# A fused top-k attention and MLP kernel: another order of the work inside each step

## Chip, cores and metric

The kernel runs on one core of one Trainium2 chip. The metric is the device time of one execution in microseconds. Before the change it is 1720.72 us, the median of three runs (1718.17 to 1720.84).

## What is computed

The reference is an attention over 64 heads (batch 8, 8 heads, 576 tokens, head size 64) that keeps only the 32 largest scores of each row, followed by an MLP with a leaky ReLU over all 4608 tokens. All of it is in float32; the MLP's weights arrive as float64 words.

```python
scores = scale * np.matmul(q, k.transpose(0, 1, 3, 2))        # 8 x 8 x 576 x 576
kth = np.partition(scores, -32, axis=-1)[..., -32:-31]
scores = np.where(scores >= kth, scores, -1000000000.0)
scores = scores - np.max(scores, axis=-1, keepdims=True)
attn = np.exp(scores)
attn = attn / (np.sum(attn, axis=-1, keepdims=True) + 1e-09)
x = np.matmul(attn, v)                       # then (B,H,S,D) -> (B*S, H*D) = 4608 x 512
h = x @ w_in                                 # 512 x 2048
out = np.maximum(0.01 * h, h) @ w_out        # 2048 x 512
```

## The kernel before

**Units.** Attention is cut into 144 units. A unit is 128 query rows of one pair of heads (both heads, 576 keys each), or the 64 rows left over in two pairs of heads. `scores` (L170) multiplies queries and keys on PE into PSUM and ACT copies the result to SBUF (`s_sb`, L186). `top_k` (L188) runs on DVE in four rounds: a round takes the eight largest of each row for both heads (two MAX8, L195) and, except in the last round, replaces them by a very low number (two MATCH_REPLACE8, L198). `mask` runs on POOL (L207 to L211): everything below the 32nd largest gets a large negative term. `exponents(u, i)` on ACT (L214) takes the exponential of head i with the row's sum; `sums` on ACT (L219, tile `ze`) adds 1e-9; `reciprocals` on DVE (L223, tile `rz`) inverts; `normalize(u, i)` on ACT (L226) multiplies head i by it. `transpose_main` (L234) and `transpose_tail` (L240) transpose the weights on PE through PSUM, with copies on ACT (L235, L241, tile `wT`). `weigh_values` (L262) multiplies by the values on PE and copies the result into the token tiles `x` (L272).

**MLP.** The tokens are cut into chunks: eight of 128 tokens, then fourteen of 256. A chunk can begin when all its units are weighed. The first product goes to `ph` (L282, 256 tokens) or `pr` (L305, 128 tokens, with transposes `pg`, L298), each in two rotating PSUM buffers that transposes and the second product share; ACT applies the leaky ReLU (Prelu, L288 or L311) into `gT`. The second product is `pz` (L333), copied by ACT (L343) and stored by a DMA on SP's queue. The MLP is written as a generator that stops every few matmuls; `mlp_steps(budget)` takes pieces from it until a budget of PE columns is used up.

**Steps.** The order of all work is written out by hand, in a loop over steps s (from L456). Step s runs the four rounds of top k for unit s (`cur`), one in each of `slot(0)` to `slot(3)`; masks and exponentials for unit s-1 (`old`); reciprocal, normalization and transposes for unit s-2 (`older`). In every odd step PE also does a group: scores for unit s+2, the values of units s-3 and s-2, scores for unit s+3. Each engine works through its own queue in this written order and waits there for what it needs from others. Seven calls of `mlp_steps` in each step, the MLP slots below, spread the MLP between these pieces. `slot_budget` divides what is ready evenly over the slots until the next chunk is ready, with a factor of 0.71 in odd steps and 1.29 in even ones.

**Start.** After the first four units there is a gap of six steps without top k (steps 4 to 9). In it `convert()` turns the weights from float64 words into float32, in 16 pieces, partly on DVE and partly on ACT; `slot(1)` to `slot(3)` begin one piece each, and beginning a piece first ends the one before the last.

Of the kernel before, what the change touches and what calls it, by code (L numbers as in the profile page):

```python
# [17 lines left out]
def kernel(  # L18
# [113 lines left out]
    def load_qk(pi):  # L132
        qt = loads.tile([P, S], F32, name="qt")
        kt = loads.tile([P, S], F32, name="kt")
        nc.sync.dma_start(qt, qT[pi])
        nc.sync.dma_start(kt, kT[pi])
        qk_of[pi] = qt, kt

    def load_v(pi):
        v_of[pi] = loads.tile([P, NKC, 2, D], F32, name="vt", bufs=LOADED_V)  # L140
        nc.sync.dma_start(v_of[pi], vk[pi])
# [28 lines left out]
    def scores(u):  # L170
        ps = [ps_sc.tile([P, 2, 512], F32, name=f"psc{i}") for i in range(2)]
        for n in range(0, len(u.parts), 2):
            for half in range(2):
                for i, pi, side, r0 in u.parts[n:n + 2]:
                    qt, kt = qk_of[pi]
                    d = slice(side * D, (side + 1) * D)
                    nc.tensor.matmul(  # L177
                        ps[i][r0:r0 + u.rows, half, 0:HS],
                        qt[d, u.q0:u.q0 + u.rows],
                        kt[d, half * HS:(half + 1) * HS],  # L180
                        start=True, stop=True,
                    )
        u.both = work.tile([P, 2, S], F32, name="s_sb", bufs=6)
        u.s = [u.both[:, i, :] for i in range(2)]
        for i in range(2):
            nc.scalar.copy(u.s[i].rearrange("p (h n) -> p h n", h=2), ps[i][:, :, 0:HS])  # L186

    def top_k(u):  # L188

        u.tops = small.tile([P, 2, ROUNDS, 8], F32, name="tops")  # L190
        rest = [work.tile([P, S], F32, name=f"rest{i}", bufs=1) for i in range(2)]
        src = u.s
        for r in range(ROUNDS):
            for i in range(2):
                nc.vector.max(out=u.tops[:, i, r, :], in_=src[i])  # L195
            if r + 1 < ROUNDS:
                for i in range(2):
                    nc.vector.match_replace(out=rest[i], in_to_replace=u.tops[:, i, r, :],  # L198
                                            in_values=src[i], imm_value=LOWEST)
                src = rest  # L200
            yield
# [11 lines left out]
    def exponents(u, i):  # L213
        nc.scalar.activation(u.s[i], u.s[i], AF.Exp, bias=u.nbias[:, i:i + 1], scale=SCALE,  # L214
                             accum_out=u.z[:, i:i + 1])

    def sums(u):
        u.ze = small.tile([P, 2], F32, name="ze")
        nc.scalar.activation(u.ze, u.z, AF.Copy, bias=1e-9, scale=1.0)  # L219

    def reciprocals(u):
        u.rz = small.tile([P, 2], F32, name="rz")
        nc.vector.reciprocal(u.rz, u.ze)  # L223

    def normalize(u, i):
        nc.scalar.activation(u.s[i], u.s[i], AF.Copy, bias=0.0, scale=u.rz[:, i:i + 1])  # L226
# [93 lines left out]
    def mlp(ch):  # L320

        n = CHUNKS[ch]
        t0 = sum(CHUNKS[:ch])
        last_turn = None
        if n == P:
            last_turn = yield from hidden_of_tile(x_of[ch])
        else:
            yield from hidden_transposed(x_of[ch], n)
        for r0 in range(0, n, P):
            pz = ps_ml.tile([P, 512], F32, name="pz", tag="ml")  # L330
            for f in range(NFC):
                need_weights(HP * DFF // WCH + f // 2 + 1)
                nc.tensor.matmul(  # L333
                    pz[:, 0:DMODEL], gT[:, f, r0:r0 + P], w_out[f // 4][:, f % 4, :],
                    start=(f == 0), stop=(f == NFC - 1),
                )
                if f == 3 and last_turn:
                    last_turn()
                    yield 4 * TRANSPOSE
                if f % 2 and f + 1 < NFC:  # L340
                    yield 2 * DMODEL
            o_sb = work.tile([P, DMODEL], F32, name="o_sb", bufs=1)
            nc.scalar.copy(o_sb, pz[:, 0:DMODEL])  # L343
            nc.sync.dma_start(out[t0 + r0:t0 + r0 + P, :], o_sb)
            yield 2 * DMODEL
# [8 lines left out]
    def mlp_steps(budget):  # L354
        owed[0] += budget
        while owed[0] > 0:
            if running[0] is None:
                if not ready:
                    owed[0] = 0.0
                    return  # L360
                running[0] = mlp(ready.pop(0))
            cost = next(running[0], None)
            if cost is None:
                running[0] = None
            else:
                owed[0] -= cost
                backlog[0] -= cost
# [14 lines left out]
    def unit(n):  # L382
        return steps[n] if 0 <= n < len(steps) else None
# [20 lines left out]
    def slot_budget(s):  # L404

        after = [at for at, _ in ready_at if at >= s]
        until = gap[-1] if s in gap else after[0] if after else s
        mean = backlog[0] / ((until + 1 - s) * SLOTS)
        if s in gap or until < s + 2:
            return mean  # L410
        return mean * (GROUPED if s % 2 else 2.0 - GROUPED)
# [5 lines left out]
    def fetch_weights():  # L417
        chunk = next(chunks, None)
        got = load_weights(*chunk) if chunk else None
        if got:  # L420
            raw_chunks.append(got)
# [6 lines left out]
    def convert():  # L428

        if len(converting) == 2 or not raw_chunks:  # L430
            for c in converting[:1]:
                next(converting.pop(0), None)
        if raw_chunks:
            begun[0] += 1
            converting.append(convert_weights(*raw_chunks.pop(0), on_vector=begun[0] % 2 == 1))
            next(converting[-1])
        fetch_weights()

    with tc.manual_schedule():
        last = {p: n for n, u in enumerate(steps) if u for p in u.pairs}  # L440
        for p in range(HP):
            load_qk(p)
            if p < 3:
                scores(units[p])
        for _ in range(3 if moe_w_in.dtype != F32 else DFF):
            fetch_weights()
        for p in range(HP):
            load_v(p)

        def load_more(s):  # L450

            for of, load, n, lag in ((qk_of, load_qk, LOADED, -2), (v_of, load_v, LOADED_V, LAG + 1)):
                while len(of) < NPAIR and (len(of) < n or last[len(of) - n] + lag <= s):
                    load(len(of))

        for s in range(len(steps) + LAG + 1):  # L456
            cur, old, older, new = unit(s), unit(s - 1), unit(s - LAG), ()
            if s % 2 and s not in gap:
                new = (units if s < FIRST else steps)[s + 2:s + 4]
            picks = top_k(cur) if cur else iter(())  # L460
            budget = slot_budget(s)

            def slot(n):
                next(picks, None)
                if s in gap and n:
                    convert()

            if older:
                reciprocals(older)
                normalize(older, 0)  # L470
                normalize(older, 1)
            slot(0)
            if old:
                mask(old, 0)
                mask(old, 1)
            mlp_steps(budget)
            mlp_steps(budget)
            if older:
                transpose_main(older, 0)
            slot(1)  # L480
            mlp_steps(budget)
            if older:
                transpose_main(older, 1)
                transpose_tail(older)
            mlp_steps(budget)
            if old:
                exponents(old, 0)
            slot(2)
            for u in new[:1]:
                scores(u)  # L490
            if s % 2:
                for u in (unit(s - LAG - 1), older):
                    if u:
                        weigh_values(u)
            for u in new[1:]:
                scores(u)
            mlp_steps(budget)
            mlp_steps(budget)
            if old:
                exponents(old, 1)  # L500
                sums(old)
            slot(3)
            mlp_steps(budget)
            attended(s)
            if s >= gap[-1]:
                load_more(s)
        mlp_steps(1e9)
# [53 lines left out]
```

## Time and profile before

| What | Before |
|---|---|
| median of three runs | 1720.72 us |
| profiled execution | 1719.7 us, its span 1717.8 us |
| mean granted clock of PE | 0.97 |
| PE busy | 1569.1 us (91%) |
| DVE busy | 1490.6 us (87%) |
| POOL busy | 1079.3 us (63%) |
| ACT busy | 1032.9 us (60%) |
| one MAX8, one MATCH_REPLACE8 | 748 ns, 743 ns |
| one exponential, one normalization | 778 ns, 769 ns |

The span reaches from the first to the last instruction; the profiled execution's own time is 1.9 us longer. A line such as "PE main L234 <- ACT s_sb L226: 78.1, 31, 12.1" says that the engine on the left waited for the one on the right 78.1 us in total, 31 times, at most 12.1 us. A line of the chain of waits says when a piece of the chain began, how long it lasted, which engine and line it was, and how many instructions it holds. In a line of the order of time the brackets hold idle time of that engine just before, and what ended it.

### The profile page before, as it was taken

How to read it: one execution, taken by the hardware profiler on the slowest of the kernel's cores; microseconds unless marked ns; L12 is line 12 of the kernel's file. 1: busy time of each engine (PE TensorE's matmuls, PEld its weight loads, DVE VectorE, ACT ScalarE, POOL GpSimd, SP SyncE). 2: the span in 40 equal slices, each digit the busy share in tenths (PEclk: the TensorE clock that was granted, in tenths of full speed). 3: DMA queues.
4: the chain of work that ended last, by engine and by line, in shares of the span. 5: the costliest groups of instructions: out<-in, count | busy, mean ns of one | idle time of the engine just before them, and what ended most of it. 6: DMA issues, size and time to landing. Idle time of an engine off the chain costs nothing.

```text
span 1717.8 us, 25394 instructions
## 1 busy us (share of the span) xinstructions
PE 1569.1 (91%) x9104; PEld 1022.0 (59%) x9104; DVE 1490.6 (87%) x3114; ACT 1032.9 (60%) x2261; POOL 1079.3 (63%) x726
## 2 busy tenths in 40 slices
PE   4454799999977999999999999999999999999999
PEld 3222455555544758585857575757576757576765
DVE  8999988888888999999998989999989899999910
ACT  4773665666665657565656565656565656566630
POOL 5205666666666676767676766676666666667720
PEclk9686899999989999999999999999999999999999
DMA  4351010100110001100110001000110010100000
GB/s 159 127 191 41 1 35 34 38 7 21 35 44 6 2 7 62 38 7 9 60 34 11 13 29 41 32 13 15 54 32 13 1 40 1 36 1 13 1 13 13
DMA packets 22462, 57.21 MB, mean 33 GB/s; under 512 B 2368, under 2 KB 2368, under 8 KB 21312
## 3 DMA queue, kind: packets, MB, share of 16 engines
q1 hardware_dynamic: 22336, 55.58, 9.5%
q8 instruction: 72, 1.18, 0.3%
q14 instruction: 54, 0.44, 0.1%
HBM read 46.14 MB, written 9.44 MB: 32 GB/s over the span
## 4 chain that ended last, share of the span: by engine, by line
PE 75%; DVE 16%; ACT 8%; DMA 1%; issue 0%; SPq 0%; ACTq 0%; DVEq 0%
PE pz L333 24%; PE ph L282 20%; PE po L262 10%; PE psc L177 10%; DVE tops L195 6%; PE main L234 6%; DVE rest L198 5%; PE pr L305 4%; ACT s_sb L226 2%; ACT wT L235 2%; PE tail L240 2%; ACT s_sb L214 1%; ACT s_sb L186 1%; DVE ex L124 1%; ACT gT L311 1%; DVE ex L110 1%
## 5 line engine op out<-in xcount | busy, mean ns | idle before, releaser
L209 POOL TENSOR_SCALAR pen<-s_sb,tops 128x576 f32<-128x576 f32 x288 | 638.5, 2217 | 440.6 <-DVE tops L195 292.6
L195 DVE MAX8 tops<-rest 128x8 f32<-128x576 f32 x864 | 609.7, 748 | 0.0
L333 PE MATMUL pz<-w_out,gT 128*128 128x512 f32 x1152 | 526.7, 601 | 13.8 <-DVE w_out L126 7.3
L198 DVE MATCH_REPLACE8 rest<-tops,rest 128x576 f32<-128x576 f32 x576 | 423.6, 743 | 0.0
L211 POOL TENSOR_TENSOR s_sb<-s_sb,pen 128x576 f32<-128x576 f32 x288 | 406.7, 1412 | 24.1
L282 PE MATMUL ph<-x,w_in 128*128 128x256 f32 x1792 | 410.9, 381 | 0.0
L282 PEld LDWEIGHTS ph<-x,w_in 128*128 128x128 f32 x1792 | 331.7, 190 | 56.2 <-issue 16.6
L333 PEld LDWEIGHTS pz<-w_out,gT 128*128 128x128 f32 x1152 | 212.5, 193 | 243.2 <-issue 223.0
L226 ACT ACTIVATE s_sb<-s_sb,rz 128x576 f32<-128x576 f32 x288 | 207.6, 769 | 109.3 <-DVE rz L223 109.3
L234 PE MATMUL main<-ident,s_sb 128*128 128x128 f32 x1152 | 177.5, 286 | 78.4 <-ACT s_sb L226 78.1
L214 ACT ACTIVATE s_sb<-s_sb,nbias 128x576 f32<-128x576 f32 x288 | 223.7, 778 | 41.3 <-POOL s_sb L211 41.2
L186 ACT COPY s_sb<-psc 128x576 f32<-128x576 f32 x288 | 169.9, 643 | 121.7 <-PE psc L177 120.6
L234 PEld LDWEIGHTS main<-ident,s_sb 128*128 128x128 f32 x1152 | 141.0, 146 | 166.0 <-ACT s_sb L226 118.5
L235 ACT COPY wT<-main 128x512 f32<-128x512 f32 x288 | 164.3, 586 | 103.0 <-PE main L234 97.9
L177 PE MATMUL psc<-kt,qt 64*128 64x288 f32 (+1 forms) x1280 | 192.8, 447 | 22.1 <-ACT s_sb L186 17.8
L198 DVE MATCH_REPLACE8 rest<-tops,s_sb 128x576 f32<-128x576 f32 x288 | 211.8, 743 | 0.0
L195 DVE MAX8 tops<-s_sb 128x8 f32<-128x576 f32 x288 | 201.7, 742 | 6.4 <-ACT s_sb L186 6.4
L262 PE MATMUL po<-wT,vt 128*64 128x128 f32 (+1 forms) x3200 | 177.8, 268 | 4.6 <-ACT wT L235 4.6
L262 PEld LDWEIGHTS po<-wT,vt 128*64 128x64 f32 x3200 | 161.2, 139 | 34.4 <-issue 20.0
L177 PEld LDWEIGHTS psc<-kt,qt 64*128 64x128 f32 (+1 forms) x1280 | 105.7, 185 | 82.2 <-issue 37.9
L223 DVE RECIPROCAL rz<-ze 128x2 f32<-128x2 f32 x144 | 22.9, 159 | 148.4 <-ACT ze L219 148.4
L288 ACT ACTIVATE gT<-ph 128x256 f32<-128x256 f32 x224 | 84.9, 379 | 102.7 <-PE ph L282 101.0
(39 smaller groups left out, 737.2 us busy)
## 6 DMA issues: line engine op xcount, KB each, us to landing
vt<-in_vk_dram SPq DMA_DIRECT2D x32, 320.0 KB, 3.9
qt<-in_qT_dram SPq DMA_DIRECT2D x32, 288.0 KB, 3.0
kt<-in_kT_dram SPq DMA_DIRECT2D x32, 288.0 KB, 3.6
out_dram<-o_sb SPq DMA_DIRECT2D x36, 256.0 KB, 2.0
raw<-in_moe_w_in_dram SPq DMA_DIRECT2D x8, 1024.0 KB, 5.1
raw<-in_moe_w_out_dram SPq DMA_DIRECT2D x8, 1024.0 KB, 4.9
```

Of the source, the lines that this page charges most:

```text
L177: nc.tensor.matmul(ps[i][r0:r0 + u.rows, half, 0:HS], qt[d, u.q0:u.q0 + u.rows], kt[d, half * HS:(half + 1) * HS], start=True, stop=True,)
L195: nc.vector.max(out=u.tops[:, i, r, :], in_=src[i])
L198: nc.vector.match_replace(out=rest[i], in_to_replace=u.tops[:, i, r, :], in_values=src[i], imm_value=LOWEST)
L209: nc.gpsimd.tensor_scalar(pen, u.s[i], u.tops[:, i, ROUNDS - 1, 7:8], MASKED, ALU.is_lt, ALU.mult)
L211: nc.gpsimd.tensor_tensor(u.s[i], u.s[i], pen, ALU.add)
L214: nc.scalar.activation(u.s[i], u.s[i], AF.Exp, bias=u.nbias[:, i:i + 1], scale=SCALE, accum_out=u.z[:, i:i + 1])
L226: nc.scalar.activation(u.s[i], u.s[i], AF.Copy, bias=0.0, scale=u.rz[:, i:i + 1])
L234: nc.tensor.transpose(main[:, c, :], u.s[i][:, k0:k0 + P], ident)
L235: nc.scalar.copy(u.wT[:, i * (NKC - 1):(i + 1) * (NKC - 1), :], main)
L262: nc.tensor.matmul(po[side * D:(side + 1) * D, o, :], vt[:, c, side, :], u.wT[:, c + side * (NKC - 1) if c + 1 < NKC else 2 * (NKC - 1), r ...
L282: nc.tensor.matmul(ph[:, 0:n], w_in[c][:, f * P:(f + 1) * P], x[c][:, 0:n], start=(c == 0), stop=(c == HP - 1),)
L333: nc.tensor.matmul(pz[:, 0:DMODEL], gT[:, f, r0:r0 + P], w_out[f // 4][:, f % 4, :], start=(f == 0), stop=(f == NFC - 1),)
```

## The change

Only the order inside a step changes. The second exponential and the sums of a unit, which stood near the end of step s-1, now open step s. The reciprocal stands behind the first round of top k instead of ahead of it. One MLP slot now stands ahead of the reciprocal, one between it and the first normalization (with the second round of top k), one between the two normalizations, and two between the second normalization and the first transposes. The second exponential, the sums and three MLP slots that stood between the group and the end of a step are gone from there, so that the odd steps end with the group.

```diff
             if older:
-                reciprocals(older)
-                normalize(older, 0)
-                normalize(older, 1)
+                exponents(older, 1)
+                sums(older)
             slot(0)
             if old:
                 mask(old, 0)
                 mask(old, 1)
             mlp_steps(budget)
+            if older:
+                reciprocals(older)
+            mlp_steps(budget)
+            slot(1)
+            if older:
+                normalize(older, 0)
+            mlp_steps(budget)
+            if older:
+                normalize(older, 1)
+            mlp_steps(budget)
             mlp_steps(budget)
             if older:
                 transpose_main(older, 0)
-            slot(1)
+            slot(2)
             mlp_steps(budget)
             if older:
                 transpose_main(older, 1)
...
             mlp_steps(budget)
             if old:
                 exponents(old, 0)
-            slot(2)
+            slot(3)
             for u in new[:1]:
                 scores(u)
             if s % 2:
...
             for u in new[1:]:
                 scores(u)
-            mlp_steps(budget)
-            mlp_steps(budget)
-            if old:
-                exponents(old, 1)
-                sums(old)
-            slot(3)
-            mlp_steps(budget)
             attended(s)
             if s >= gap[-1]:
                 load_more(s)
```

## Prediction

> **What bounds the kernel now.** I read the page's slices first, then busy time by stretches, then the waits of PE by stretch, then the chain and the order of time in the stretches that lose time.
>
> Page, section 2 (busy tenths and granted clock in 40 slices of 43 us):
>
> ```profile
> PE   4454799999977999999999999999999999999999
> ...
> DVE  8999988888888999999998989999989899999910
> ...
> PEclk9686899999989999999999999999999999999999
> ```
>
> Three regimes: to about 200 us DVE is full and PE half empty (top k of the first units, then the weight conversions); near 450 to 560 us PE dips; the rest is PE's. Busy time by stretches puts numbers on it:
>
> ```profile
> 193.50:450.00 256.50, 246.04 (x1381) 136.04 (x1380) 221.06 (x475) 159.63 (x349) 171.05 (x114) 1.00 0.08 27
> 450.00:560.00 110.00, 89.88 (x495) 52.68 (x493) 95.31 (x206) 65.52 (x143) 73.50 (x50) 0.92 0.08 23
> 560.00:1645.00 1085.00, 1069.73 (x6555) 733.44 (x6555) 993.68 (x2139) 685.07 (x1569) 763.33 (x511) 1.00 0.07 23
> ```
>
> Columns: length, then busy PE, weight load, DVE, ACT, POOL. PE idles 10.5, 20.1 and 15.3 us there, DVE 35, 15 and 91. From 193.5 us on PE's work is fixed, so only its 46 us of idle time can be won, and every us by which that phase starts later is lost in full. DVE's largest wait is therefore no measure of the gain. Waits, whole span:
>
> ```profile
> DVE rz L223 <- ACT ze L219: 148.4, 89, 8.1
> ...
> PE main L234 <- ACT s_sb L226: 78.1, 31, 12.1
> ```
>
> The second is what the change aims at: PE's transposes waiting for a normalization. The same wait by stretch (before 200, 200 to 450, 450 to 560, 560 to 1650):
>
> ```profile
> PE main L234 <- ACT s_sb L226: 48.4, 9, 12.1
> ...
> PE main L234 <- ACT s_sb L226: 2.5, 2, 1.4
> ...
> PE main L234 <- ACT s_sb L226: 18.6, 7, 4.6
> ...
> PE main L234 <- ACT s_sb L226: 8.6, 13, 1.0
> ```
>
> **The change, part by part.** No instruction is added or removed, and seven MLP slots stay seven. SP's queue keeps its order: output stores go with the MLP pieces, weight fetches with the conversions, loads at the end of a step. Write P for the time at which PE enters a step and R for its reciprocal. From an even step's R to the next DVE needs 9.8 us (chain: four max pairs of 1.32, three replacement pairs of 1.46, the reciprocal), for instance 468.52 to 478.33.
>
> *Before*, R waits for ze, issued one MLP slot before the step ends, and the transposes come two slots after the step begins. A pair of steps is about 22 us; less the group (1.17 + 2.33 + 1.17) and two sets of transposes (1.0 each) it leaves 15.3 us in 14 slots: 1.09 each, by the factors 0.71 and 1.29 some 0.78 us in odd steps and 1.41 in even. So an odd step gives ACT and DVE 1.41 + 2 x 0.78 = 3.0 us for second exponential, ze, reciprocal and first normalization (0.9 + 0.25 + 0.2 + 0.8 = 2.15), after whatever Prelu is in front. As the MLP comes in pieces of 0.86 to 1.72 us, two short slots can hold none; then PE waits, as at 632 us (1.03 us, both transpose sets back to back).
>
> *After*, five slots (3.9 us odd, 7 us even) lie between P and the first transpose. Even: two score copies 1.06, exponential 0.9, ze 0.25, hence R = P + 2.6, normalization done by P + 3.6. Odd: R is set by DVE, 9.8 us after the even one; with an even step of 10.9 us (7 x 1.41 + 1.0) that is P + 1.5, normalization done by P + 2.5, while the smallest content of five odd slots is two pieces, 3.4 us. So these waits vanish from 196 us on: the one at 196.8 (1.36), the two at 253.8 and 276.1 (1.35 + 1.20) and the 8.6 of the long stretch: **-12.5 us**. The waits of the tail transpose (0.24 us each) stay, since one slot still lies between the two sets.
>
> *The dip* (450 to 560 us) has little MLP work, and the loop through all engines sets it. Chain of waits:
>
> ```profile
> 500.23 0.08 DVE rz L223
> 500.33 0.79 ACT s_sb L226
> ...
> 501.16 1.97 PE main L234 x8
> ...
> 503.43 2.22 PE psc L177 x8
> 505.65 3.00 PE po L262 x40
> 508.65 1.17 PE psc L177 x8
> 509.82 1.93 PE pr L305 x4
> 511.77 0.60 ACT gT L311
> 512.37 0.76 ACT s_sb L214 x2
> ```
>
> Odd R to even R takes 12.1, 13.2, 12.4, 12.5 us (mean 12.5); the other half is DVE's 9.8. Without MLP work the same loop took 11.0 (164.2 to 175.2). The excess is MLP pieces of slots 3 to 6 inside the loop. After the change only slots 6 and 7 lie inside; PE does the others while it waits for R. PE was busy for 70 us in 470 to 560; less 10 us of attention in each of four pairs, 30 us remain, 7.5 a pair, 0.54 a slot, 0.38 in odd steps, so 0.75 us for two: 11.75 instead of 12.5, times four turns: **-3.1 us** (bounds: 0 if pieces fall badly, -11 if DVE's 9.8 alone sets it).
>
> On clock: eight transposes took 1.97 us after 7.4 us of idle, 1.97 after 3.36, 1.79 after 2.75, and 1.04 warm; I leave this premium in place, as 2.75 us was enough to pay it. The Trainium skill, "TensorE: Matmul & The Clock Gate", Part 1, puts the drop to half clock behind an idle window of about 3.4 us; by it, gaps a little shorter would stay warm and save about another 1 us a turn, an estimate of 4 us in all. The 1.79 row speaks against that.
>
> *The start* is the price. While DVE is the bound, a reciprocal behind a round makes everything that hangs on it a round (1.31 + 1.46 = 2.8 us) later. Order of time, before:
>
> ```profile
> 47.80 0.20 ACT L219 ACTIVATE ze<-z 128x2 f32<-128x2 f32 x1
> ...
> 48.03 0.17 DVE L223 RECIPROCAL rz<-ze 128x2 f32<-128x2 f32 x1 [1.96 <-ACT ze L219]
> ...
> 60.44 0.17 DVE L223 RECIPROCAL rz<-ze 128x2 f32<-128x2 f32 x1 [0.57 <-ACT ze L219]
> ```
>
> Step 3's reciprocal moves from 36.3 to 39.1, so its normalization, group and the second exponential of unit 2 follow 2.8 later and the reciprocal at 48.0, which stands ahead of the first conversion on DVE, goes to 50.8. Then the gap: the second exponential of unit 3 was issued before the third conversion, and is now behind it, on an ACT queue that holds, from 53.6 on: first conversion 2.15, two normalizations 1.4, transposes and copy 1.0, second conversion 4.4, two copies 0.8, first exponential 1.0, third conversion 2.15, second exponential and ze 1.15. That ends at 67.5, and DVE's next reciprocal, with the rest of the conversions queued behind it, goes from 60.4 to 67.5: **+7.1 us**. DVE is then busy without a break until 135, so this stays. When top k resumes (units 4, 5), the reciprocal again stands a round later: **+2.8 us**. PE's full phase starts 9.9 us later. Bounds: +5.6 if ACT catches up in the gap, +12 if the late first chunk also holds a conversion.
>
> *ACT's queue* gets a wait ahead of MLP work: the normalization waits for R, and behind it stand the Prelus, for which PE waits when both PSUM buffers are full; at an even step's start the Prelu stands behind copies, exponential and ze until P + 2.6. A hidden tile takes 8 x 0.216 = 1.73 us, so PE reaches the third tile at P + 2.6 at the earliest: just covered. With 128-token chunks the next tile follows after four transposes (0.44 us); there I charge 14 tiles x 0.15 x 0.7 = **+1.5 us**. If the cover fails, see below. POOL: both masks take 7.3 us from the last round; the second exponential now comes later still, so no wait.
>
> **Sum.** 9.9 + 1.5 - 12.5 - 3.1 = -4.2 us on the profiled execution (span 1717.8, run 1719.7): 1715.5. The run lies 1.0 under the median of 1720.72 and inside the runs' 1718.17 to 1720.84; I say 1716.
>
> **Rivals.**
> - *The ends cancel* (about 1720). The start costs its 9.9, and half of the 15.6 us comes back: DVE-bound odd steps in the 128-column phases still wait, and the dip keeps its loop. For it: the terms are each few us, known to some 2. Against: five slots exceed the need in each case that I worked out.
> - *ACT becomes PE's wait* (slower). Mechanism: at the start of each even step the first Prelu ends at P + 2.6 and PE's third hidden tile wants its buffer at 2.6. If ACT is later than I read (a leftover Prelu, copies waiting 0.1 longer for the second score), half of the 49 pairs after 560 us (1085 / 22), those that begin in the hidden phase, lose it; at 0.6 us that is +15 us, 1731. It decides from 0.3 us on: 25 x 0.3 = 7.5 takes the 4.2 back and passes the 3.4 that can be told. For it: the margin is nil by my own numbers; against: it needs a tile left half done by the step before, and copies now start 0.04 to 0.1 us after the scores end.
> - *The loop goes free* (faster, 1705). The dip falls to DVE's 9.8 a step (-11) and the gap's queue catches up (+5.6): about -16. For it: DVE's 148 us of waits; against: the dip's loop holds 11.0 us without any MLP piece.
> - *Nothing reaches the end*: DVE's waits move but PE is full anyway, which is the first rival with the start left out; the start shift makes it unlikely.
>
> **How the numbers follow.** Forecast 0.40, loop free 0.06, ends cancel 0.24, slower 0.30 (ACT's wait 0.20, the start's price without the gains 0.10, about 1728). A measurement of this kernel can tell about 0.2%, 3.4 us, from no change: faster 0.46, same 0.24, slower 0.30. Range 1704 to 1731: below, the free loop; above, most of ACT's wait. The forecast's own range is 1710 to 1719.
>
> **What would show it.** Right: PE's waits for L226 after 200 us near 15 us instead of 30, nearly all in the dip; odd-to-even turns there near 11.8; DVE's wait for ze far below 148 after 560 us; the second reciprocal of the gap at about 67, the last conversion at about 142, PE full from about 203. Wrong: new PE waits on gT L288 or L311 of 0.3 us and more at even steps (ACT's wait); conversions that end by 138 (start dearer on paper than on the chip); L226 waits of 1 us that recur each chunk as before.

## The result and the profile after

The changed kernel takes 1727.72 us (median of four runs, 1726.70 to 1728.58) against 1719.99 us before: a ratio of 1.0046, 95% interval [1.0029, 1.0064]. It is slower by 8 us, where 4 us less were forecast. The span of its profiled execution is 1726.4 us against 1717.8.

The page's slices after the change (busy tenths, and granted clock, in 40 slices of 43 us):

```profile
PE   4363699999977999999999999999999999999999
...
DVE  8799988888898899999999998989898989898910
...
PEclk9677799999988999999999999999999999999999
```

The shape is the same: DVE's start, the dip in the twelfth and thirteenth slice, the long full stretch of PE. Busy time by stretches, with the stretches moved by the 10 us by which PE's full phase now begins later (length, then PE, weight load, DVE, ACT, POOL; the last figures are the granted clock, the DMA share and GB/s):

```profile
203.50:460.00 256.50, 249.33 (x1398) 139.29 (x1397) 223.45 (x481) 160.11 (x352) 171.02 (x116) 1.00 0.08 27
460.00:570.00 110.00, 89.05 (x495) 54.63 (x494) 94.61 (x206) 63.96 (x143) 73.90 (x50) 0.88 0.08 23
570.00:1655.00 1085.00, 1060.63 (x6537) 728.89 (x6536) 988.01 (x2127) 677.08 (x1563) 763.44 (x509) 1.00 0.07 23
```

PE idles 7.2, 21.0 and 24.4 us there, against 10.5, 20.1 and 15.3. The waits, over the whole span and then PE's wait for the normalization by stretch (to 210, to 460, to 580 us, and the rest), and last, for comparison, the kernel before after 580 us:

```profile
DVE rz L223 <- ACT ze L219: 160.0, 78, 7.3
...
PE main L234 <- ACT s_sb L226: 101.2, 36, 17.7
```

```profile
PE main L234 <- ACT s_sb L226: 63.6, 8, 17.7
...
PE main L234 <- ACT s_sb L226: 0.8, 1, 0.8
...
PE main L234 <- ACT s_sb L226: 20.4, 6, 5.3
...
PE main L234 <- ACT s_sb L226: 16.5, 21, 1.5
```

```profile
PE main L234 <- ACT s_sb L226: 7.8, 12, 1.0
```

So the wait that the change is aimed at grew from 78.1 to 101.2 us. It grew at the start, where that was forecast, and it shrank from 2.5 to 0.8 before the dip, also as forecast. In the dip it did not fall (18.6 before, 20.4 now). After the dip it doubled, from 7.8 (after 580 us) to 16.5, where it was to vanish. From the beginning of PE's full phase to the end the kernel now takes 1522.9 us (203.5 to 1726.4) against 1524.3 (193.5 to 1717.8). The loss is the start, 10.0 us; the gain that should have outweighed it came out at 1.4 us.

The start in order of time (DVE's reciprocals in and before the gap):

```profile
39.15 0.16 DVE L223 RECIPROCAL rz<-ze 128x2 f32<-128x2 f32 x1
51.07 0.17 DVE L223 RECIPROCAL rz<-ze 128x2 f32<-128x2 f32 x1 [4.89 <-ACT ze L219]
67.87 0.17 DVE L223 RECIPROCAL rz<-ze 128x2 f32<-128x2 f32 x1 [5.53 <-ACT ze L219]
```

The forecast had 39.1, 50.8 and 67.5.

### The profile page after: what moved, and what is told of

It reads as the page before. It is cut to its first block, busy times and chain, and to the rows that moved or that the text cites. A ratio compares the mean times of both kernels' runs of the same rounds, so it can differ in the third digit from the quotient of the medians.

```text
span 1726.4 us, 25382 instructions
## 1 busy us (share of the span) xinstructions
PE 1563.1 (91%) x9104; PEld 1023.8 (59%) x9104; DVE 1488.4 (86%) x3114; ACT 1024.5 (59%) x2261; POOL 1079.0 (62%) x726
## 4 chain that ended last, share of the span: by engine, by line
PE 69%; DVE 21%; ACT 9%; issue 0%; DMA 0%; SPq 0%; ACTq 0%
PE pz L333 24%; PE ph L282 14%; PE po L262 10%; PE psc L177 10%; DVE tops L195 9%; DVE rest L198 8%; PE main L234 5%; PE pr L305 5%; ACT s_sb L186 2%; ACT s_sb L214 2%; ACT wT L235 2%; ACT s_sb L226 2%; PE tail L240 1%; DVE ex L124 1%; DVE ex L110 1%; DVE w_in L126 1%
## 5 line engine op out<-in xcount | busy, mean ns | idle before, releaser
L226 ACT ACTIVATE s_sb<-s_sb,rz 128x576 f32<-128x576 f32 x288 | 210.4, 768 | 111.2 <-DVE rz L223 111.2
L234 PE MATMUL main<-ident,s_sb 128*128 128x128 f32 x1152 | 175.7, 286 | 101.2 <-ACT s_sb L226 101.2
L234 PEld LDWEIGHTS main<-ident,s_sb 128*128 128x128 f32 x1152 | 145.0, 147 | 183.9 <-ACT s_sb L226 121.7
L288 ACT ACTIVATE gT<-ph 128x256 f32<-128x256 f32 x224 | 84.3, 376 | 95.9 <-PE ph L282 95.4
```

What stands on the lines that cost most here:

```text
L234: nc.tensor.transpose(main[:, c, :], u.s[i][:, k0:k0 + P], ident)
```

## The experiments

### Where the loss is: four hybrids

Two theories. A: the start costs all of it, in two terms, the gap and the resumption of top k. B: the later steps cost it. The first three kernels hold both step bodies (the order of work inside a step) and choose by step; a second exponential that the other body has already done is not done twice.

```diff
+            if s < 16:        # e1; "s >= 16" in e2, "s < 6" in e3
+                ...           # the step of before
+            else:
+                ...           # the changed step
```

> The order of before in steps 0 to 15, the changed order from step 16 on. Theory A (the start costs all of it: PE's full phase begins 10.0 us later in the changed kernel, 203.5 against 193.5 us, and from there both orders take the same, 1522.9 against 1524.3 us): full phase from 193.5 us, time near 1718 to 1720, ratio to before 0.999 to 1.000. Rival B (the later steps cost it: PE's waits for normalizations after 580 us rose from 7.8 to 16.5 us, and the late start is made good further on): full phase from 193.5 us, yet 1726 to 1728, ratio 1.004.

> The mirror of the other one: the changed order in steps 0 to 15, the order of before from step 16 on. Theory A: full phase from 203.5 us, time 1729 to 1731, ratio 1.005 to 1.006. Rival B: 1720 to 1722, ratio 1.000 to 1.001.

> The order of before only in steps 0 to 5 (all steps with attention work before or in the gap of the conversions), the changed order from step 6 on. Theory A with its two terms (7.1 us from the reciprocal at 67.9 instead of 60.4 us, 2.8 us from the round ahead of the reciprocal when top k resumes): last conversion ends at 135.3 us as before, full phase from 196.3 us, time 1721 to 1723, ratio 1.001. If the first term is all of the start's cost, full phase from 193.5 us and 1718 to 1720; rival B: 1726 to 1728.

The fourth is the changed step with one edit:

```diff
                 exponents(older, 1)
                 sums(older)
+                reciprocals(older)
             slot(0)
...
             mlp_steps(budget)
-            if older:
-                reciprocals(older)
             mlp_steps(budget)
```

> The changed order, with only the reciprocal put back ahead of the first round of top k (behind the second exponential and the sums of the same step). Theory A: the two rounds at the start come back (2 x 2.8), the reciprocal behind the third conversion does not; second reciprocal of the gap near 65 us, full phase from 198 us, and the later steps as in the changed kernel, since a turn from one reciprocal to the next holds four rounds in either place: 1721 to 1723, ratio 1.001. Rival C (the round ahead of the reciprocal gives DVE the slack that the change is about, so without it DVE waits at each step for the sums): the mean turn of an even and an odd step together, 21.4 us now, grows by 1 us and more, time 1760 and above.

| Kernel | us | Ratio to before | Interval |
|---|---|---|---|
| e1, start of before, then changed | 1718.18 | 0.9987 | 0.9979 to 0.9996 |
| e2, changed start, then before | 1729.67 | 1.0050 | 1.0037 to 1.0062 |
| e3, before to step 5, then changed | 1720.43 | 1.0002 | 0.9993 to 1.0011 |
| e4, reciprocal first | 1722.05 | 1.0013 | 1.0004 to 1.0022 |

e1, e2 and e4 fall where theory A put them; e3 is 0.6 us below its own range (1721 to 1723), and far from theory B's. With the start of before, the changed steps are some 2 us faster than before; with the changed start, the old steps are some 9 us slower. By the times the start costs 9.5 us (1727.72 against e1's 1718.18). e3 gives back 7.3 of them, which is the gap's term (7.1 forecast). The other 2.3 lie in steps 6 to 15, where the round ahead of the reciprocal at the resumption was put at 2.8. The second reciprocal of the gap shows the terms one by one, first in e1, then in e4 (order of time, DVE):

```profile
60.50 0.17 DVE L223 RECIPROCAL rz<-ze 128x2 f32<-128x2 f32 x1 [0.57 <-ACT ze L219]
```

```profile
64.89 0.17 DVE L223 RECIPROCAL rz<-ze 128x2 f32<-128x2 f32 x1 [4.93 <-ACT ze L219]
```

e4 says something else besides: in the later steps the place of the reciprocal among the rounds is worth nothing. PE's wait after 580 us is 16.4 us with it first and 16.5 with it behind a round, and the mean even and odd turns (from an even or an odd step's reciprocal to the next, between 650 and 1600 us) agree to 0.01 us: 9.79 and 11.57 against 9.79 and 11.58. Four rounds lie between one reciprocal and the next in either place.

### Where the gain went: the loop, the budgets, the pieces

PE's largest waits for a normalization after 580 us are six of 1.49 us, 8.9 of the 16.5 us. Each stands in the last step before a chunk of 256 tokens is ready, in six of the thirteen chunks that become ready there. The other fifteen, of 0.27 to 0.64 us, stand in other steps. One of the six, in order of time:

```profile
711.69 1.24 PE L177 MATMUL psc<-kt,qt 64*128 64x288 f32 x8
...
715.17 0.17 DVE L223 RECIPROCAL rz<-ze 128x2 f32<-128x2 f32 x1 [3.00 <-ACT ze L219]
...
716.40 0.60 PE L234 MATMUL main<-ident,s_sb 128*128 128x128 f32 x4
...
718.55 0.60 PE L234 MATMUL main<-ident,s_sb 128*128 128x128 f32 x4
...
719.10 5.32 PE L333 MATMUL pz<-w_out,gT 128*128 128x512 f32 x12
...
724.89 0.15 DVE L223 RECIPROCAL rz<-ze 128x2 f32<-128x2 f32 x1
...
725.91 0.66 PE L234 MATMUL main<-ident,s_sb 128*128 128x128 f32 x4 [1.49 <-ACT s_sb L226]
```

The group ends at 712.9. The even reciprocal comes 2.3 us later, DVE's four rounds set the odd one 9.7 us after that, and the normalization is done 1.0 us later: 13.0 us after the group. PE is at the odd transposes at 724.4, after only 11.5 us. It had two pieces in the five even slots where the prediction counted 7 us, and three pieces in the last even and the five odd slots together. A cause that the code suggests is this line of `slot_budget`:

```python
if s in gap or until < s + 2:
    return mean
```

In the last two steps before a chunk is ready the factors 0.71 and 1.29 are not used, and the even step is short. Here `s` is the step and `until` the one in which the next chunk becomes ready. Two theories, then, and a third from the pieces of 1.72 us to which every slot is rounded: L, the loop through group, copies, second exponential and sums makes the even reciprocal late; M, the budgets of those two steps; P, the size of the pieces.

e5 takes the second exponential out from behind the group; e6 also puts the reciprocal first:

```diff
-            if older:
-                exponents(older, 1)
-                sums(older)
             slot(0)
...
             if old:
                 exponents(old, 0)
+                exponents(old, 1)
+                sums(old)
             slot(3)
```

> The changed order, but the second exponential and the sums are issued right behind the first exponential, ahead of the group, instead of at the start of the next step. Theory L (the loop: from the odd reciprocal through normalization, transposes, group, the copies of the second scores, second exponential and sums to the even reciprocal, 11.0 us without any MLP piece, after which DVE's 9.7 us follow; the change left this loop as it was, so PE still meets a late normalization): with the exponential out from behind the group the odd turn falls from 11.6 to about 10, PE's waits for normalizations after 460 us fall from 36.9 to under 10 us, the dip's pairs from 22.2 to about 20 us, full phase from about 196 us; time 1698 to 1708, ratio 0.988 to 0.993. Rival M (uneven slot budgets: the last two steps before a chunk are not grouped, so even steps there are too short): waits of 1.5 us once a chunk remain, time 1718 to 1724. Rival Q (ACT's queue: a second exponential that waits for POOL's mask holds up the score copies): the group waits, 1728 and more.

> As the one with the second exponential ahead of the group, and the reciprocal ahead of the first round of top k. Theory L: with the sums early, the reciprocal waits for nothing in either place, so the later steps are as in that run, and the start gains a round each time (2.8 us at the resumption of top k): 1 to 4 us less than that run. Rival C (the round ahead of the reciprocal is the slack that counts): 5 us or more above it.

e7 and e8 use the factors in every step outside the gap, in the changed kernel and in the one before:

```diff
-        if s in gap or until < s + 2:
+        if s in gap:
             return mean
```

> The changed order, with the budget factors 0.71 and 1.29 in all steps, also in the last two before a chunk is ready, where the kernel uses 1. Rival M: the 1.5 us waits vanish, PE's waits for normalizations after 580 us fall from 16.5 to under 6 us, time 1716 to 1720 (the start's loss stays). Theory L: an even budget only moves pieces from inside the loop's odd turn (slots 6 and 7) to outside, so half of the waits go: 1721 to 1725.

> The control for the one above: the order of before with the same budgets in all steps. Rival M: the 1.0 us waits vanish, 7.8 us after 580 us fall to about 2, time 1714 to 1717. Theory L: in this order four slots lie inside the odd turn instead of two, so moving pieces to the even step gains at least as much: 1712 to 1717. If the exception was there for a reason (a chunk's pieces left over when the next is ready): 1722 and more.

e12 halves the pieces of the 128-token first product and of the second product, in the changed kernel:

```diff
-                if c == 1:
-                    yield 2 * 512
+                if c + 1 < HP:
+                    yield 512
...
-                if f % 2 and f + 1 < NFC:
-                    yield 2 * DMODEL
+                if f + 1 < NFC:
+                    yield DMODEL
```

> The changed kernel with the MLP pieces of the 128-token first product and of the second product cut to half (0.86 us instead of 1.72). Theory P (size of the pieces: the dip's odd turns alternate between 11.8 and 13.1 us because slots 6 and 7 hold either no piece or a whole one, and the late normalizations come from whole pieces that fall on the wrong side): dip turns all near 12.2, PE's waits for normalizations after 580 us from 16.5 to under 6 us, time 1710 to 1718. Rival M (the uneven budgets of the last two steps): those waits stay between 12 and 18 us, the turns even out without a gain, time 1724 to 1728.

| Kernel | us | Ratio to before | Interval | PE's wait for L226 after 580 us |
|---|---|---|---|---|
| e5, second exponential ahead of the group | 1690.65 | 0.9829 | 0.9815 to 0.9842 | 1.5 |
| e6, and reciprocal first | 1693.15 | 0.9844 | 0.9830 to 0.9857 | 1.5 |
| e7, changed, factors everywhere | 1699.87 | 0.9885 | 0.9870 to 0.9900 | 3.0 |
| e8, before, factors everywhere | 1710.85 | 0.9947 | 0.9934 to 0.9959 | 4.2 |
| e12, changed, halved pieces | 1690.90 | 0.9832 | 0.9818 to 0.9847 | 0.8 |

Each of the three edits alone takes most of these waits away: of 16.5 us e5 leaves 1.5, e7 3.0 and e12 0.8. All three times, and e8's, lie below what was expected. e7 still has two waits of 1.49 us, each in the last step before a chunk. And these waits are not the whole gain: at the 43rd of the 144 reciprocals, just behind the dip, e5 is already 21.4 us ahead of the changed kernel (564.7 against 586.1 us; 7.9 of that is the start, as PE's full phase begins at 195.6 us), e7 14.4 and e12 9.2. PE's largest waits after 580 us, in e7 and then in e12:

```profile
PE tail L240 <- ACT wT L235: 8.4, 35, 0.2
PE main L234 <- ACT s_sb L226: 3.0, 2, 1.5
```

```profile
PE tail L240 <- ACT wT L235: 2.4, 10, 0.2
PE main L234 <- ACT s_sb L226: 0.8, 3, 0.3
```

The theories are therefore not rivals: they are three terms of one inequality. PE must not be at the odd transposes before the even reciprocal plus 9.7 plus 1.0 us. e5 makes the reciprocal earlier, e7 gives PE more to do in between, e12 lets the slots hold what the budgets say. No theory stands alone: M's forecast for e12, waits of 12 to 18 us, fell, and so did its forecast for e5 and L's for e7. e5 shows the loop directly: the odd turn (from an odd reciprocal to the next) falls from 11.58 to 9.78 us on average between 650 and 1600 us, DVE's rounds alone, and it is the even turn that now has slack (11.22 us, from 9.79).

e6 missed both expectations: its first reciprocal of PE's full phase (192.5 instead of 196.2 us) is 3.7 us earlier than e5's, yet it is 2.5 us slower. In the dip its PE waited 5.5 us for the score copies, which e5 did not, and its lead fell from 2.2 us (31st reciprocal) to 0.8 (43rd). By the last reciprocal it was 1.8 us behind, though both kernels show the same waits for normalizations after 580 us. So the copies explain the dip at most; what costs e6 the other 2.6 us stays open.

Sums of these edits:

> The second exponential ahead of the group and the budget factors in all steps, together. If both remove the same thing (PE coming to the odd normalization before DVE's four rounds have ended, since even steps are too short or the even reciprocal too late), little is left after the first of the two: PE's waits for normalizations after 580 us were 1.5 us with the exponential moved, so 1687 to 1692. If they remove different waits they add up: 1670 to 1680.

> As the one before, with the reciprocal ahead of the first round of top k in steps 0 to 15 only. The start's term alone: full phase 2.8 to 3.7 us earlier, time 2 to 4 us below that run. If the start's rounds are made good elsewhere: the same time as that run.

> The changed order from step 16 on, the order of before in steps 0 to 15, and the budget factors in all steps. If start and budgets are independent, the two effects add: 1699.9 less 9.5 gives 1688 to 1692. If an earlier start only gives more waiting later: 1695 to 1700.

They took 1685.23, 1682.79 and 1691.91 us (ratios 0.9799, 0.9785 and 0.9837, each within 0.0017). e9 lies between its two ranges, e10 and e11 in the ranges of added effects. Exponential and budgets add up to a part only: after 580 us either alone leaves little of the waits for normalizations, and together they leave none. The start's term adds on top: 2.4 us for its round (e10 against e9), and 8 us for the whole of it (e11 against e7).

### Is the order worth anything after the start?

Small pieces might help any order. The last three runs settle it: halved pieces in the order of before, in the changed order with the start of before, and in the version that joins e10 with them.

> The order of before with the MLP pieces halved. Theory H (the order's gain is real and was hidden by whole pieces): the order of before, which has two short slots ahead of the odd transposes, keeps waits for normalizations, and four slots inside the odd turn keep the turn long: 1700 to 1712. Theory G (small pieces help any order alike, since slots are then as even as the budgets say): 1681 to 1687, as much below 1719.5 as the changed kernel fell, 37 us.

> The changed order from step 16 on, the order of before in steps 0 to 15, pieces halved. The start's 10 us come off the 1690.9 us of the changed order with halved pieces: 1679 to 1684. Against the order of before with halved pieces: Theory H 18 to 30 us less, Theory G within 4 us.

> Second exponential ahead of the group, budget factors in all steps, reciprocal ahead of the first round in steps 0 to 15, pieces halved. The parts overlap: after 580 us nothing is left of the waits for normalizations already with whole pieces, and the waits of the tail transposes (8.4 us by the view) go with small pieces: 1668 to 1678, if the dip's 11.5 us stay.

| Kernel | us | Ratio to before | Interval |
|---|---|---|---|
| e13, before, halved pieces | 1702.15 | 0.9898 | 0.9885 to 0.9912 |
| e14, start of before, then changed, halved pieces | 1680.81 | 0.9775 | 0.9762 to 0.9788 |
| e15, all joined, halved pieces | 1680.29 | 0.9773 | 0.9759 to 0.9786 |

PE's waits for the normalization after 580 us, e13 and then e14:

```profile
PE main L234 <- ACT s_sb L226: 10.3, 22, 0.7
```

```profile
PE main L234 <- ACT s_sb L226: 0.8, 3, 0.3
```

With halved pieces the changed order is 21.3 us faster than the old one after the same start; with whole pieces the difference was 2.2 us (e1). Theory H stands: the order's gain is real and whole pieces hid it. It lies wholly after the dip: the 43rd reciprocal comes at 568.1 us in e13 and at 568.0 in e14. Halved pieces alone help the old order too, by 18 us (e13), and not by these waits, which grew there from 7.8 to 10.3 us.

e15 missed its expectation of 1668 to 1678. The dip is not the reason: its waits, 12.8 us, are about what the expectation allowed for. At the 43rd reciprocal e15 is 5.7 us ahead of e14 (562.25 against 567.96 us), and by the last it is 0.9 us behind. The waits of the tail transposes after 580 us, which were to go, are 4.8 us, twice the 2.4 of e14; the rest of that loss was not traced. e14 and e15 are the fastest here and equal within their intervals.

## Why the prediction was wrong

- **The start, +9.9 us**: right, in place and about right in size. The gap's second reciprocal was put at 67.5 and came at 67.87, the full phase at about 203 and came at 203.5. The second exponential behind the third conversion on ACT and the round ahead of the reciprocal are both shown by e3 and e4. In other runs of the same start (e2, e7, e12) the reciprocal came at 65.8 and the full phase at 201.0 to 201.6, so some 2 us of the term vary from run to run, and the agreement to 0.1 us is partly luck.
- **The waits that "vanish from 196 us on", -12.5 us**: this step failed. Of its parts, the 3.9 us before the dip came (0.8 left). The 8.6 us of the long stretch (7.8 after 580 us) became 16.5. The working took an even step of 10.9 us and two pieces in five odd slots for every pair. But the last two steps before a chunk is ready have no factors, which the working left out, and pieces are whole: in the place shown the five even slots held 3.4 us instead of 7, and PE was at the odd transposes 11.5 us after the group, where the normalization took 13.0. The even reciprocal at P + 2.6 was about right (2.3 to 2.4 after 580 us), and so was DVE's 9.8 (9.7); the content of the slots was not, and an average of budgets cannot show it. e7 and e12, which change only that content, show that it decides. One of the prediction's own signs of being wrong appeared: waits that recur at the ends of chunks as before, six of 1.49 us, against six of about 1.03.
- **The dip, -3.1 us**: this failed too, by what the two slots inside the loop hold. The odd turns were forecast at 11.75 us; they alternate, 13.0 and 11.7 (mean 12.4), against 12.5 before, so the four turns gained some 0.6 us. In the chain of waits of the changed kernel:

```profile
508.12 0.08 DVE rz L223
...
510.17 3.41 PE pr L305 x4
...
521.12 0.17 DVE rz L223
...
530.92 0.08 DVE rz L223
...
542.66 0.17 DVE rz L223
```

  The first of the two odd turns shown (508.12 to 521.12) holds one whole piece, which took 3.41 us instead of 1.72, at a granted clock of 0.88 over the dip; the other (530.92 to 542.66) holds none. I had charged 0.75 us for both slots. With halved pieces (e12) the four turns are 11.0, 11.3, 12.6 and 11.6, mean 11.6.
- **ACT's queue, +1.5 us, and the slower rival (ACT becomes PE's wait)**: neither came. PE's waits for gT between 200 and 460 us are 3.1 us against 3.4 before, none stands on L288, and the longest single one on L311 is 0.40 us against 0.35.
- **The direction** failed because the one large gain was counted in full and the start was right. Without the start, the sum's other terms are -14.1 us; 1.4 us came. The branch of "the start's price without the gains" had about 1728 and a chance of 0.10; it is what happened. "The loop goes free" was a real possibility, but of another edit: e5.
- **Clock**: I kept the premium for transposes at a low clock in place, and the trace agrees. The longest wait in the dip grew from 4.6 to 5.3 us, four of the six there are over 4 us, and the granted clock there fell from 0.92 to 0.88. The transposes after 4.3 to 5.3 us of idle ran slow (1.97 us for eight, 1.11 for four), and those after 1.10 us did not (0.66 for four). The Trainium skill, "TensorE: Matmul & The Clock Gate", Part 1, puts the drop to half clock behind an idle window of about 3.4 us. The rows above agree with that; the kernel before does so only in part. There eight transposes took 1.97 us after 3.36 us of visible idle time and 1.79 after 2.75, but 1.33 after 3.34, so a stretch somewhat below the window can pay or not.

What e12's 37 us are made of: PE's waits after 580 us, as the view shows them, fall by only 20.5 us (15.7 of L226, 4.8 of the tail). Counted from the start of one PE instruction to the start of the next, beyond the usual time of the first, more is seen. From the 43rd to the last reciprocal the kernel takes 1042.2 us instead of 1071.8. Of these 29.6 us, 18 stood between MLP work and transposes and 8 between main and tail transposes (the last section tells why the view shows less). Between 250 us and the 43rd reciprocal e12 gains 9.4 us, 6.4 of them between main and tail transposes. What stays open is some 7 us of it, most of what e6 loses against e5, and most of what e15 loses against e14.

## What to carry to other kernels

When two engines run in lockstep through a loop of steps, write down for each sync point what must have happened before what, and check it in the worst step (the shortest, with slots rounded to whole pieces of work and with the exceptions of the planner), not with the mean slot. Ask of an edit whether it takes something out of the loop or only moves the point at which the loop is cut: the reciprocal behind a round moved the cut and cost two rounds at the start, while the exponential ahead of the group shortened the loop by what stood behind it. And cost the start of a pipeline by itself; there the slack that the steady state has does not exist yet.

## What the runs showed that I had not expected

PE's visible idle time understates a stall, as the ends of matmuls are modelled: the four transposes at 716.40 us are shown as 0.60 us long, yet the next row of PE begins 0.44 us after them, at 716.84. When no piece falls between the two sets of transposes, the tail transpose waits for a copy. The waits view shows 0.24 us for it; the chain of waits of the changed kernel shows more:

```profile
466.74 0.45 PE main L234 x4
467.21 0.59 ACT wT L235
...
467.85 0.33 PE tail L240
468.18 1.72 PE pz L333 x4
```

The second set of transposes runs beside the copy and is not in the chain. In the 1.44 us from 466.74 to 468.18 PE does two sets and the tail, which need 0.44 + 0.44 + 0.11 = 0.99 us where a piece of the MLP hides the copy. So about 0.45 us are lost where the view shows 0.24. After 580 us this happened 30 times in the changed kernel and 10 times with halved pieces: at 0.45 us each a difference of some 9 us (an estimate), instead of 4.8.
